# Scale columns and K projection in three chunks of three k-tiles, with the first layer norm's statistics reordered, in a diffusion transformer block

## The chip, the cores and the metric

One core of a Trainium2 chip runs the whole block as one program. The metric is device microseconds for one execution. The kernel before took 243.84 us (median of 3, 243.79 to 243.88). Chips and executions differ by some tenths of a microsecond, so each kernel was run beside the kernel before on the same chip. A profile adds the **span**, from the core's first instruction to its last. It is shorter than the time.

## The reference

```python
B, N, D = (2, 256, 1152);  F = 4 * D;  H = 2
mod = (silu(c) @ w_mod).reshape(B, 6, 1, D)
shift_a, scale_a, gate_a, shift_m, scale_m, gate_m = [mod[:, i] for i in range(6)]
h = layernorm(x) * (1 + scale_a) + shift_a
qkv = (h @ wqkv).reshape(B, N, 3, H, D // H)
...                                   # softmax attention, two heads
x = x + gate_a * (attn_out @ wo)
h2 = layernorm(x) * (1 + scale_m) + shift_m
return x + gate_m * (gelu(h2 @ w_fc1) @ w_fc2)
```

All tensors are bf16. D is 9 tiles of 128 ("k-tiles" as the contracted dimension). The 512 tokens are four tiles of 128, two for each batch element.

## The kernel before

Everything is recorded as units of work with their dependencies, and each engine runs its own queue in order. TensorE (PE) runs the units in the order in which the program states them; lists fix the first instructions of VectorE (DVE), ScalarE (ACT) and, in the changed kernel, GpSimd.

The stage in question is the first 34 us. It computes K before the shift is known: K of the scaled, unshifted rows. (The shift's part of K adds the same amount to all scores of a query, so softmax drops it.) The steps are: normalise four token tiles, transpose them on PE, compute the scale columns `silu(c) @ w_mod` as many matmuls of two columns, multiply (`hk`), and project. The scale weights come in chunks so that K can start on the first ones:

```python
KC = 4
for (ka, kb) in ((0, KC), (KC, KT)):            # scale columns 0..3, then 4..8
    for k0, k1 in ((0, 3), (3, 6), (6, 9)):
        dma(WSC[:, k0:k1, ka*P:kb*P], wmod_v[:, k0:k1, D + ka*P:D + kb*P], ...)
    for kt in range(ka, kb):
        dma(WK[:, kt, :], ...)
...
warm(7, "b")                                    # identity x zeros, 512 columns: keeps PE busy
for n, behind in ((1, "bn_ln1_1_1"), (1, "aggr_ln1_1"), (2, "veps_ln1_1"), (2, "rstd_ln1_1")):
    warm(n, behind, behind)                     # may start only after the named DVE or GpSimd step
xn_T(1)                                         # transposes of tile 1
sca(0, 3);  warm(1, "d");  sca(3, 6);  warm(1, "f", "aggr_ln1_2")
xn_T(0);  sca(6, 9);  xn_T(2, 0, 8)
...
k_pair(range(KT - 2), 3, 1, bank=1)             # the last pair of K columns, k-tiles 0..6
for k0 in range(0, KT, 3): ...                  # shift rows: silu(c) @ W_shift
copy_on("dve", SHR, ...)                        # their eviction
k17(0, KC, KT);  k17(1, 0, 2)                   # seven K matmuls beside it
...                                             # transpose the shift rows into columns (shT)
k_pair(range(KT - 2, KT), 3, 1, bank=1)         # the last pair's k-tiles 7, 8: four matmuls
k17(1, 2, KT)                                   # seven more; then Q, which needs the shift added
```

## Time and profile before

| | before |
|---|---|
| time | 243.84 us |
| time / span of the profiled run | 244.31 / 242.6 us |
| PE busy | 238.3 us, 98% of the span |
| tile 1 normalised / its transposes start on PE | 7.91 / 8.62 us |
| first K matmul | 11.55 us |
| first Q matmul | 33.20 us |

The lines are in the prediction. Note that the profiled run is a separate one, 0.47 us slower than the median; that matters below, too. A "start us, us" line of the chain gives start and length of a piece; in a timeline, "[0.28 <-X]" is idle time of the engine ahead of the instruction and what ended it. The first Q matmul is 0.216 us (one matmul of 512 columns) ahead of the first one recorded: its record is missing, while its weight load is there.

### The profile page before, as it was taken

The numbers are of one execution on the slowest core, as the hardware profiler recorded it, in microseconds if no ns is written. First come the engines' busy times: TensorE is split into PE (matmuls) and PEld (weight loads), VectorE is DVE, ScalarE is ACT, GpSimd is POOL, SyncE is SP. The second block draws the span as 40 slices with busy tenths as digits, with TensorE's granted clock in tenths as the row PEclk, the third lists the DMA queues.
The fourth block names the chain that finished last, engine by engine and source line by source line (L and its number), as shares of the span: only waits on it lengthen the run. The fifth ranks groups of instructions, "written<-read, shape, count | busy, mean of one in ns | idle before, by whom it ended". The sixth has DMA issues, their size and how long they took to land.

```text
span 242.6 us, 3989 instructions
## 1 busy us (share of the span) xinstructions
PE 238.3 (98%) x1717; PEld 146.4 (60%) x1727; DVE 120.0 (49%) x216; ACT 66.9 (28%) x136; POOL 21.7 (9%) x39
## 2 busy tenths in 40 slices
PE   7999999999999999999999999999999999999996
PEld 2688854557667666898444444444565665665664
DVE  3824379596988799789999600000012222211112
ACT  4730350345424207983233332222000000000000
POOL 1500000000021186400000000020000000000000
PEclk9999999999999999999999999999999999999999
DMA  6999999999994999999943488002000000000001
GB/s 237 330 383 394 388 392 389 397 412 408 390 355 138 349 385 393 390 320 394 329 145 87 165 301 331 0 16 85 0 16 19 16 16 19 16 16 16 19 17 32
DMA packets 29995, 51.57 MB, mean 213 GB/s; under 512 B 1431, under 2 KB 15643, under 8 KB 29979
## 3 DMA queue, kind: packets, MB, share of 16 engines
q1 hardware_dynamic: 29536, 50.14, 57.8%
q0 software_dynamic: 416, 1.19, 1.6%
q8 instruction: 13, 0.21, 0.4%
q14 instruction: 3, 0.02, 0.0%
q10 hardware_dynamic: 27, 0.00, 0.0%
HBM read 50.14 MB, written 1.19 MB: 212 GB/s over the span
## 4 chain that ended last, share of the span: by engine, by line
PE 98%; issue 0%; POOL 0%; DVE 0%; POOLq 0%
PE psum L688 96%; PE psum L691 2%; POOL arena L713 0%; DVE arena L1289 0%; DVE arena L1290 0%; POOL arena L712 0%; POOL arena L719 0%; POOL arena L717 0%; POOLq L1351 0%
## 5 line engine op out<-in xcount | busy, mean ns | idle before, releaser
L688 PE MATMUL psum<-arena 128*128 128x384 bf16 (+9 forms) x1628 | 235.0, 310 | 2.0 <-POOL arena L713 1.5
L688 PEld LDWEIGHTS psum<-arena 128*128 128x128 bf16 (+1 forms) x1638 | 141.1, 97 | 91.8 <-issue 4.7
L1081 DVE SCALAR_TENSOR_TENSOR arena<-arena 128x1152 f32<-128x1152 bf16 x32 | 44.7, 1413 | 0.6
L1289 DVE TENSOR_TENSOR arena<-psum,arena 128x384 f32<-128x384 f32 (+2 forms) x13 | 6.9, 527 | 68.3 <-PE psum L688 68.3
L1197 ACT ACTIVATE arena<-psum 128x512 bf16<-128x512 f32 (+1 forms) x44 | 22.4, 519 | 42.7 <-PE psum L688 42.7
L683 ACT ACTIVATE arena<-psum 128x512 bf16<-128x512 f32 (+6 forms) x37 | 19.5, 549 | 39.8 <-PE psum L688 38.5
L685 DVE CAST arena<-psum 128x512 bf16<-128x512 f32 (+3 forms) x13 | 8.1, 639 | 11.5 <-PE psum L688 11.5
L669 POOL DMA_DIRECT2D dit_scratch<-arena x3 | 1.8, 616 | 116.4 <-DVE arena L685 59.6
L1165 POOL TENSOR_TENSOR arena<-arena 128x384 f32<-128x384 f32 x12 | 10.9, 912 | 10.9 <-DVE arena L1164 9.3
L1108 DVE CAST arena<-psum 72x32 bf16<-72x32 f32 x1 | 0.2, 188 | 21.3 <-PE psum L688 21.3
L741 DVE BATCH_NORM_STATS2 arena<-arena 128x6 f32<-128x384 f32 (+1 forms) x18 | 9.5, 551 | 0.1
L1170 ACT ACTIVATE arena<-arena 128x1152 bf16<-128x1152 f32 x4 | 5.3, 1343 | 11.3 <-DVE arena L1169 11.3
L1164 DVE TENSOR_TENSOR arena<-psum,arena 128x384 f32<-128x384 f32 x12 | 6.5, 550 | 1.3 <-PE psum L688 1.2
L691 PEld LDWEIGHTS psum<-arena 128*128 128x128 bf16 (+1 forms) x89 | 5.9, 98 | 2.1 <-DMA arena<-in_c_dram 0.8
L691 PE MATMUL psum<-arena 128*128 128x128 bf16 (+1 forms) x89 | 7.1, 219 | 0.1
L1290 DVE TENSOR_TENSOR arena<-arena 128x384 bf16<-128x384 f32 (+2 forms) x13 | 6.9, 527 | 0.4
L1187 ACT ACTIVATE arena<-psum,arena 128x128 bf16<-128x128 bf16 x16 | 6.0, 455 | 1.5 <-PE psum L691 0.9
L1184 DVE TENSOR_SCALAR arena<-psum,arena 128x128 bf16<-128x128 bf16 x20 | 5.4, 336 | 1.9 <-PE psum L691 1.9
L1085 DVE STREAM_TRANSPOSE arena<-arena 128x1152 f32<-128x1152 f32 x4 | 5.5, 1368 | 0.0
L1088 DVE TENSOR_REDUCE arena<-arena 128x36 f32<-128x1152 f32 x4 | 5.4, 1346 | 0.0
L1011 ACT ACTIVATE arena<-psum,arena 128x256 bf16<-128x256 f32 x8 | 3.7, 472 | 1.3 <-PE psum L688 0.9
L745 POOL TENSOR_TENSOR arena<-arena 128x1 f32<-128x1 f32 x6 | 3.6, 596 | 1.6 <-DVE arena L744 1.6
(48 smaller groups left out, 45.3 us busy)
## 6 DMA issues: line engine op xcount, KB each, us to landing
arena<-in_w_fc_dram SPq DMA_DIRECT2D x9, 1152.0 KB, 7.1
arena<-in_w_fc_dram SPq DMA_DIRECT2D x4, 2592.0 KB, 17.4
arena<-in_wqkv_dram SPq DMA_DIRECT2D x18, 288.0 KB, 9.7
arena<-in_w_mod_dram SPq DMA_DIRECT2D x3, 1728.0 KB, 20.5
arena<-in_w_mod_dram SPq DMA_DIRECT2D x3, 864.0 KB, 13.0
arena<-in_w_mod_dram SPq DMA_DIRECT2D x9, 288.0 KB, 11.1
arena<-in_wqkv_dram SPq DMA_DIRECT2D x1, 2592.0 KB, 16.9
arena<-in_wo_dram SPq DMA_DIRECT2D x1, 2592.0 KB, 24.4
```

The source lines that it names most:

```text
L683: act(c_act(n), lambda e: e.activation(out=dst, in_=src, func=ACTF.Copy), [src], [dst], name)
L685: dve(c_dve_psum16(n) if psum16 else c_dve_psum32(n), lambda e: e.tensor_copy(dst, src), [src], [dst], name)
L688: S.instr(lambda e: e.matmul(o, lhsT=l, rhs=r, start=st, stop=sp, **kw), reads=[l, r], writes=[o])
L691: S.instr(lambda e: e.transpose(o, i_, idn), reads=[i_, idn], writes=[o])
L741: dve(550, lambda e, s=s, o=o: e.bn_stats(out=o, in_=s), [s], [o], "bn_%s_%d" % (tag, ci))
L1081: dve(1270, lambda e, w=w, s=s, acc=acc: e.scalar_tensor_tensor(out=acc, in0=w, scalar=s, in1=acc, op0=ALU.mult, op1=ALU.add), [w, s, acc] ...
L1164: dve(550, lambda e, o=o, ga=ga, x1c=x1c: e.tensor_tensor(out=x1c, in0=o, in1=ga, op=ALU.mult), [o, ga], [x1c], "wo_t1_%d_%d" % (t, ci))
L1165: S.op("pool", 930, lambda e, xs=xs, x1c=x1c: e.tensor_tensor(out=x1c, in0=x1c, in1=xs, op=ALU.add), reads=[x1c, xs], writes=[x1c], name=" ...
L1187: act(440, lambda e, o=o, dst=dst, s1=s1, s2=s2: e.activation(out=dst, in_=o, func=ACTF.Identity, scale=s1, bias=s2), [o, s1, s2], [dst], ...
L1197: act(c_act(ntok), lambda e: e.activation(out=dst, in_=o, func=ACTF.Gelu_apprx_tanh), [o], [dst], "gelu_%d_%d" % (f, tok0))
L1289: dve(c_dve_psum32(w), lambda e, o=o, gm=gm, t1=t1: e.tensor_tensor(out=t1, in0=o, in1=gm, op=ALU.mult), [o, gm], [t1], "fc2_t1_%d_%d" % ( ...
L1290: dve(c_dve_32(w), lambda e, t1=t1, x1c=x1c, ost=ost: e.tensor_tensor(out=ost, in0=t1, in1=x1c, op=ALU.add), [t1, x1c], [ost], "fc2_out_%d ...
```

## The change

The intent: smaller pieces, so that K can start earlier; tile 2's statistics ahead of all normalising, so that the three tiles are normalised in one go; and the last K pair ahead of the shift rows, whose weights arrive late.

```diff
-KC = 4
+KC = 3
-        for (ka, kb) in ((0, KC), (KC, KT)):
+        for (ka, kb) in ((0, KC), (KC, 2 * KC), (2 * KC, KT)):
...
-        for n, behind in ((1, "bn_ln1_1_1"), (1, "aggr_ln1_1"), (2, "veps_ln1_1"), (2, "rstd_ln1_1")):
+        for n, behind in (..., (2, "rstd_ln1_1"), (1, "bn_ln1_2_1"), (2, "bn_ln1_2_2")):
             warm(n, behind, behind)
+        sca(0, 3)
         xn_T(1)
-        sca(0, 3)
-        warm(1, "d")
         sca(3, 6)
-        warm(1, "f", "aggr_ln1_2")
         xn_T(0)
...   # one ACT copy of transposes more; the second half of the scale columns becomes two thirds,
...   # the last of them between the K matmuls of k-tile 5
         k_pair(range(KT - 2), 3, 1, bank=1)
+        k_pair(range(KT - 2, KT), 3, 1, bank=1)
...   # shift rows, eviction
         k17(0, KC, KT)
-        k17(1, 0, 2)
+        k17(1, 0, 1)
...   # shT
-        k_pair(range(KT - 2, KT), 3, 1, bank=1)
-        k17(1, 2, KT)
+        k17(1, 1, KT)
...
-            "dve": [..., "bn_ln1_2_1", "xn_1", "bn_ln1_2_2", "aggr_ln1_2", "veps_ln1_2", "xn_0", "var_ln1_3", "xn_2", ...
+            "dve": [..., "bn_ln1_2_1", "bn_ln1_2_2", "aggr_ln1_2", "veps_ln1_2", "xn_1", "xn_0", "xn_2", "var_ln1_3", ...
+            "pool": [..., "rstd_ln1_2", "mm_ln1_3", "rstd_ln1_3"],
```

More of the change, by code (lines that the diff above doesn't have):

```diff
@@ L801, in hk @@
             dst = HK[:, kt, b * 256:(b + 1) * 256]
-            s1 = ps32(1 if kt == 0 else 7, 2 * kt, 1) if kt in (0, KC) and b == 0 else SC1A[:, kt * 2 + b:kt * 2 + b + 1]
+            s1 = ps32(1 if kt == 0 else 7, 2 * kt, 1) if kt % KC == 0 and b == 0 else SC1A[:, kt * 2 + b:kt * 2 + b + 1]
             src = xslot(b, kt) if kt < KC else HX[:, kt, b * 256:(b + 1) * 256]
@@ L852, in build_kernel @@
         warm(7, "b")
-        for n, behind in ((1, "bn_ln1_1_1"), (1, "aggr_ln1_1"), (2, "veps_ln1_1"), (2, "rstd_ln1_1")):
+        for n, behind in ((1, "bn_ln1_1_1"), (1, "aggr_ln1_1"), (2, "veps_ln1_1"), (2, "rstd_ln1_1"), (1, "bn_ln1_2_1"), (2, "bn_ln1_2_2")):
             warm(n, behind, behind)
+        sca(0, 3)
         xn_T(1)
-        sca(0, 3)
-        warm(1, "d")
         sca(3, 6)
-        warm(1, "f", "aggr_ln1_2")
         xn_T(0)
@@ L868, in build_kernel @@
         xn_T_copy(0, 8, 9, "act")
+        xn_T_copy(0, 3, 4, "act")
         hk(2, 0, "act")
-        hk(3, 0, "act")
         def k_first(kt):
@@ L885, in build_kernel @@
             hk(kt, 1)
+        xn_T_copy(1, 3, 4, "dve")
         k_pair(range(KC), 0, 1)
-        k_pair(range(KC), 1, 1)
         def k17(b, ka, kb):
@@ L896, in build_kernel @@
         k17(0, 0, KC)
-        def k12(part):
-            kts = ((range(3), ()), (range(3, KC), range(KC)))[part]
-            S.unit("pe", sum(map(len, kts)) * c_mm(256), "k1_2_part%d" % part)
-            for half in range(2):
-                k_mm(kts[half], 4 + half, 1, KB[1][2], half)
         for kt in range(KT):
             if kt == 6:
-                k12(0)
-            mod_kt(WSC, kt, 0, "scb_%d" % kt, (KC, KT))
+                k_pair(range(KC), 1, 1)
+            mod_kt(WSC, kt, 0, "scb_%d" % kt, (KC, 2 * KC))
         hk(KC, 0)
-        sc1a(KC, KT)
-        for kt in range(KC, KT):
+        sc1a(KC, 2 * KC)
+        for kt in range(KC, 2 * KC):
             for b in range(2):
@@ L912, in build_kernel @@
                     hk(kt, b)
-        k12(1)
+        k_pair(range(KC), 2, 1)
+        for kt in range(KC, 2 * KC):
+            for b in range(2):
+                if kt == 2 * KC - 1:
+                    for k in range(6 * b, 6 + 3 * b):
+                        mod_kt(WSC, k, 0, "scc_%d" % k, (2 * KC, KT))
+                for i in range(4 - b):
+                    k_pair((kt,), i, b)
         for kt in range(KT):
@@ L916, in build_kernel @@
             dma(WSM[:, kt, :], wmod_v[:, kt, 4 * D:5 * D], P * D * 2, "ld_sm%d" % kt, run=2304)
-        for kt in range(KC, KT - 2):
+        hk(2 * KC, 0)
+        sc1a(2 * KC, KT)
+        for kt in range(2 * KC, KT):
             for b in range(2):
-                for i in range(4 - b):
-                    k_pair((kt,), i, b)
+                if kt > 2 * KC or b:
+                    hk(kt, b)
+        for b in range(2):
+            for i in range(4 - b):
+                k_pair((2 * KC,), i, b)
         for b in range(2):
@@ L974, in build_kernel @@
             "dve": ["zq4b", "c_half", "c_silu", "bn_ln1_1_0", "bn_ln1_1_1", "bn_ln1_1_2", "aggr_ln1_1", "veps_ln1_1", "bn_ln1_2_0",
-                    "bn_ln1_2_1", "xn_1", "bn_ln1_2_2", "aggr_ln1_2", "veps_ln1_2", "xn_0", "var_ln1_3", "xn_2", "hk_0_0", "sc1a_0", "sc1a_1", "hk_1_0", "xn_3",
-                    "hk_0_1", "hk_1_1", "hk_2_1", "hk_3_1", "hk_%d_0" % KC, "sc1a_4", "hk_%d_1" % KC] + ["hk_%d_%d" % (kt, b) for kt in range(KC + 1, KT) for b in range(2)],
-            "act": ["ld_c", "c_tanh", "sum_ln1_0", "sq_ln1_0", "sum_ln1_3", "sq_ln1_3", "xnT_cp0_4", "xnT_cp0_8", "hk_2_0", "hk_3_0",
+                    "bn_ln1_2_1", "bn_ln1_2_2", "aggr_ln1_2", "veps_ln1_2", "xn_1", "xn_0", "xn_2", "var_ln1_3", "hk_0_0", "sc1a_0", "sc1a_1", "hk_1_0",
+                    "xn_3", "hk_0_1", "hk_1_1", "hk_2_1", "xnT_cp1_3"]
+                   + [x for kt in range(KC, KT) for b in range(2) for x in (["hk_%d_%d" % (kt, b)] + (["sc1a_%d" % kt] if kt % KC == 0 and b == 0 else []))],
+            "act": ["ld_c", "c_tanh", "sum_ln1_0", "sq_ln1_0", "sum_ln1_3", "sq_ln1_3", "xnT_cp0_4", "xnT_cp0_8", "hk_2_0", "xnT_cp0_3",
                     "xnT_cp1_4", "xnT_cp1_8"],
+            "pool": ["ones", "ident", "nhalf", "rowpad0", "rowpad640", "mm_ln1_0", "rstd_ln1_1", "var_ln1_0", "rstd_ln1_0", "rstd_ln1_2",
+                     "mm_ln1_3", "rstd_ln1_3"],
         }
```

## The prediction

> **What bounds the kernel now.** I read the page first, then the chain of work that ended last in order of time, then the timeline of the first 35 us engine by engine, then DMA issues in narrow windows. The page says that PE carries everything:
>
> ```profile
> PE 238.3 (98%) x1717; PEld 146.4 (60%) x1727; DVE 120.0 (49%) x216; ACT 66.9 (28%) x136; POOL 21.7 (9%) x39
> ...
> PE 98%; issue 0%; POOL 0%; DVE 0%; POOLq 0%
> ```
>
> The change touches only the first 34 us: LN1, the scale columns, the K projection, the shift rows. There the chain (start us, length us, what) never leaves PE after 1.5 us:
>
> ```profile
> 4.96 3.82 PE psum L688 x11
> 8.78 0.50 PE psum L691 x9
> 9.29 0.83 PE psum L688 x25
> 10.11 0.08 issue
> 10.19 0.66 PE psum L691 x9
> 10.85 0.29 PE psum L688 x12
> 11.14 0.47 PE psum L691 x8
> 11.61 1.95 PE psum L688 x16
> 13.56 0.56 PE psum L691 x10
> 14.12 19.24 PE psum L688 x234
> ```
>
> The lines of L691 are the transposes of the normalised tiles; the x11 before them are warm-up matmuls (identity times zeros, 512 columns). So PE is busy before 8.6 us too, with work that computes nothing. Does it wait for LN1 at 8.62, where the first transpose starts? The DVE timeline says no:
>
> ```profile
> 6.43 1.01 DVE L741 BATCH_NORM_STATS2 arena<-arena 128x6 f32<-128x384 bf16 x2
> 7.35 0.56 DVE L762 TENSOR_SCALAR arena<-arena 128x1152 bf16<-128x1152 bf16 x1
> 7.83 0.55 DVE L741 BATCH_NORM_STATS2 arena<-arena 128x6 f32<-128x384 bf16 x1
> 8.42 0.24 DVE L742 BATCH_NORM_AGGREGATE arena<-arena 128x2 f32<-128x18 f32 x1
> 8.69 0.15 DVE L744 TENSOR_SCALAR arena<-arena 128x1 f32<-128x1 f32 x1
> 8.76 0.57 DVE L762 TENSOR_SCALAR arena<-arena 128x1152 bf16<-128x1152 bf16 x1
> ```
>
> L762 is the normalising of a tile: tile 1 is ready at 7.91, tile 0 at 9.33. PE takes them at 8.62 and 10.19. It comes late because its queue of warm-ups, each of them released long before, has to be run off first. Half of them run at the cold spacing (7.32 to 7.74, the weight loads 0.42 us apart):
>
> ```profile
> 7.32 0.15 PEld L688 LDWEIGHTS psum<-arena 128*128 128x128 bf16 x1 [0.28 <-DVE arena L741]
> 7.74 0.55 PEld L688 LDWEIGHTS psum<-arena 128*128 128x128 bf16 x3 [0.28 <-issue]
> ```
>
> So in this stretch **the end is set by the sum of PE's matmuls plus the few places where PE stands still**. From the start-to-start distances of single PE records after 8.62 us, what exceeds the usual distance is: 0.11 us at 11.55 (first K matmul; its K weights landed at 11.42), 0.04 at 12.24 (an ACT copy), 0.06 at 12.53 (next K weights), 0.12 at 20.10 (the first scaled tile of the second chunk), 0.05 at 31.76 (the eviction of the shift rows). A step of about 0.21 us at 10.19 and 33.41 is a matmul whose record is missing (1717 matmuls to 1727 loads), not a wait.
>
> **What the Trainium skill says.** "TensorE: Matmul & The Clock Gate", section "Wait — 56ns, not 53.3ns?": start to start is N/1.2 GHz while cold (426.7 ns for 512 columns) and N/2.4 plus 2.5 ns when warm (215.7 ns for 512, 55.6 for 128), never under about 25 ns. The trace agrees: 0.43 us cold, nine transposes in 0.50 us, 512-column warm-ups 215 ns apart after 7.97, two-column matmuls 26.5 ns apart, 256-column ones 109 ns. The same page, "What's actually happening", puts the change to full clock in a free-running window; the three runs within 0.09 us show no such scatter here. "DMA: Bandwidth & Descriptors", section "Specifications", asks for 512 B at least for line rate; the trace agrees only in part: the first scale chunk (1024 B rows) moves at 294 GB/s, the later weights (2304 B rows) at 392:
>
> ```profile
> 5.00:9.30 4.30, 4.30 (x27) 1.99 (x26) 4.16 (x12) 4.24 (x7) 2.47 (x6) 1.00 0.95 294
> ...
> 18.00:29.00 11.00, 11.00 (x136) 9.77 (x135) 4.88 (x17) 2.39 (x4) 0.00 (x0) 1.00 1.05 392
> ```
>
> **The change part by part.**
>
> *Warm-ups.* Out: "d" and "f", one each. In: one behind the second statistics part of tile 2 and two behind the third. The DVE finishes these at 7.44 and, with the normalising moved behind, about 7.9; PE reaches them at 8.62, so they start at once. Net one more matmul of 215 ns: **+0.215 us**. They all stand before the first useful matmul now, so scale columns start at 8.62 + 3 x 0.215 = 9.27.
>
> *Statistics of tile 2 first.* On DVE, third part at 7.35, aggregate and epsilon until 8.36, then the tiles 1, 0, 2 normalised until about 8.85, 9.4, 9.9. PE wants them at 9.51, 10.25, 10.99 (below). All come 0.6 us or more early: **0**. The gain that the reordering makes possible is eaten by the three warm-ups.
>
> *Three scale chunks instead of two.* The 81 two-column matmuls stay; nine of them (9 x 26.5 = 0.24 us) move from before the first K matmul to later: no change of the sum. PE then: 9.27 scale k 0..2 (9 x 26.5), 9.51 transposes tile 1 (0.50), 10.01 scale, 10.25 tile 0, 10.75 scale, 10.99 eight transposes of tile 2, 11.43 free. First scaling on DVE: now 0.25 us after the last first-column matmul (10.74 to 10.99), so 10.80 + 0.25 = 11.05, plus 0.36, plus 0.06 to PE: K starts at 11.47, a wait of 0.04. The ACT copies of the transposes start 0.26 us after the last transpose of tile 0, so 10.95, 0.06 later than now; the banks they free are wanted 0.08 us earlier: waits of 0.12 and 0.05 for the third and fourth K pair. The second K tile starts at 12.52, where it now starts at 12.53. Weights come sooner here, as the first chunk is 885 KB instead of 1180, so the 0.06 at 12.53 goes. Later: the scale ones wait for the last ACT copy of tile 3's transposes, about 0.04; the 0.12 at 20.10 goes down to about 0.01 at each of two places, because six K matmuls (0.65 us) stand there where five did.
>
> *Last K pair ahead of the shift rows.* Seven matmuls cover the rows' eviction as before. But after the transposing of the rows only 8 matmuls (0.87 us) stand before Q, where 11 (1.20 us) did. Shift columns and first two additions took from 32.01 to 32.94, plus 0.06 to PE, so 0.99 us: **a new wait of 0.12 us**.
>
> *Transfers.* Rows of scale weights shrink to 768 B: 3456 of them instead of 2304, so 216 per DMA engine instead of 144. From the rates, a 1024 B row cost 56 ns per engine and a 2304 B row 94. I take 42 ns for a 768 B row, an estimate between proportion to size from the smooth stretch (34) and no saving at all (56). 216 x 42 = 9.1 us against some 8.0 now: every later landing about 1 us later. The last shift weights landed at 28.96 and are used at 30.26; K's extra pair pushes the use 0.44 us on. The last Q weights land at 41.7 and are used at about 43.4; 42.8 still suffices. **0, with little to spare.**
>
> Sum of PE: +0.215 (one warm-up), minus the old waits that go (0.11 + 0.04 + 0.06 + 0.12 = 0.33), plus the new ones (0.04 + 0.17 + 0.04 + 0.02 + 0.12 = 0.39): **+0.28 us**. After Q nothing waits on anything but PE, so it is passed on whole: 243.84 + 0.28 = 244.1 us.
>
> **The rivals.** *The new order wins.* If the three new warm-ups only filled time in which PE would wait for the statistics, leaving out "d" and "f" (0.43 us) would count, and with the wait at 20.10 gone the time would be about 243.3. For it: that is the evident intent. Against: no warm-up now waits, and tile 1 would be normalised 0.65 us before PE wants it. *The short rows starve PE.* At 56 ns a row the stream is 4 us later; PE would wait for the third scale chunk (wanted at about 21) and for the last Q weights: 245 to 246.5. For it: the slow first chunk and a DMA busy without a gap until 58 us. Against: median rows in the trace are near proportional to size, and the slow part is the first microseconds. *A copy chain becomes the bound*: ACT has one copy more before tile 3's transposes, but it ends near 13.1 and the next need is at 14.15; I see at most 0.2 us more, 244.3.
>
> **Range and chances.** The sum is of terms of 0.05 to 0.2 us, each uncertain by half, so about 0.3 us either way; the first rival draws the low end, a part of the second the high end: 243.4 to 244.8. Two per cent is 4.9 us, more than all waits and warm-ups of the stage, so within 2% is all but sure: 0.98, with 0.01 on either side.
>
> **What would show it.** Three warm-ups 0.215 us apart between 8.62 and 9.27, then two-column matmuls; first K matmul at 11.4 to 11.6; no PE wait near 20; Q starting about 0.3 us later than the 33.2 of now; the last scale rows landing around 20 us. A first K matmul well before 11.4 would refute the warm-up count; PE waiting on a weights transfer anywhere would refute the DMA step.

## The result, and the profile after

The changed kernel took **244.38 us** (median of 4, 244.26 to 244.58); the kernel before, beside it, 243.86 (4 runs). The ratio is 1.0021, 95% interval 1.0003 to 1.0038. A ratio here is the mean of one kernel's fast runs over that of the other's in the same rounds, so not quite the ratio of the medians. The class is "same", and the time lies in the predicted range; the middle of the difference is 0.52 us where 0.28 was predicted.

The page of the changed kernel, engines' busy time and then the chain's shares, looks as before:

```profile
PE 238.2 (98%) x1719; PEld 146.4 (60%) x1728; DVE 120.5 (50%) x219; ACT 67.0 (28%) x136; POOL 21.2 (9%) x39
...
PE 98%; DVE 1%; issue 0%; POOL 0%; POOLq 0%
```

The chain of work in order of time, first stage:

```profile
4.88 4.26 PE psum L688 x23
9.15 0.63 PE psum L691 x9
9.78 0.22 PE psum L688 x9
9.99 0.52 PE psum L691 x9
10.52 0.21 PE psum L688 x9
10.73 0.47 PE psum L691 x8
11.20 1.97 PE psum L688 x16
...
32.93 0.29 DVE arena L972
33.22 0.08 issue
33.29 0.81 PE psum L688 x3
```

Two things are as foretold: transposes and two-column matmuls alternate in groups of nine, and a DVE line (L972, adding the shift) now stands in the chain ahead of Q. One is not: K starts near 11.1, well ahead of the predicted 11.47; by the prediction's own sign ("a first K matmul well before 11.4") that refutes its warm-up count. The timeline of PE's weight loads and the timeline of DVE say why:

```profile
6.38 0.15 PEld L688 LDWEIGHTS psum<-arena 128*128 128x128 bf16 x1 [0.28 <-DVE arena L741]
6.81 2.24 PEld L688 LDWEIGHTS psum<-arena 128*128 128x128 bf16 x17 [0.28 <-DVE arena L744]
9.10 0.51 PEld L691 LDWEIGHTS psum<-arena 128*128 128x128 bf16 x9
```

```profile
6.63 1.47 DVE L741 BATCH_NORM_STATS2 arena<-arena 128x6 f32<-128x384 bf16 x3
8.13 0.24 DVE L742 BATCH_NORM_AGGREGATE arena<-arena 128x2 f32<-128x18 f32 x1
8.40 0.15 DVE L744 TENSOR_SCALAR arena<-arena 128x1 f32<-128x1 f32 x1
8.47 1.71 DVE L762 TENSOR_SCALAR arena<-arena 128x1152 bf16<-128x1152 bf16 x3
```

PE went over from 0.43 to 0.22 us a warm-up: the first one at full rate starts at 7.0 us, not at 8.0 as in the trace of before. So the warm-ups were through at 8.77 and the first nine scale matmuls at 9.01, and PE then stood still for 0.09 us until tile 1 was normalised (9.04). The warm-ups are not what bounds this run up to here; LN1 on DVE is.

The transfers: with 768 B rows the scale weights moved faster than expected. The second and third piece of the first chunk, 24 rows for each of the 16 DMA engines, landed 0.88 us after the one before: 37 ns a row where 42 was assumed. The windows view (the last two columns are DMA share and GB/s) has, for a stretch that holds the end of the token load (landed at 6.17) and most of the first chunk, and for the later weights:

```profile
5.20:9.30 4.10, 4.10 (x27) 1.89 (x26) 3.96 (x12) 4.04 (x7) 2.25 (x5) 1.00 1.04 355
...
20.00:29.00 9.00, 9.00 (x105) 8.07 (x104) 4.10 (x13) 2.39 (x4) 0.00 (x0) 1.00 1.06 391
```

The last scale rows landed at 20.15, the last Q weights at 42.29 against 41.74 before: 0.55 us later, and PE waits for none of them.

**A puzzle.** PE's last weight load is at 240.03 in this trace and at 240.15 in that of before. PE ends 0.12 us earlier, yet the span is 243.1 instead of 242.6. (The two profiled runs took 244.37 and 244.31 us: this pair of traces differs by 0.06 us in time, not by 0.52.) The difference in span lies behind the last matmul. Of the last store (16 KB; us from issue to landing in the last column) the two traces say, first before, then changed, where an instruction transfer also falls into the same window:

```profile
out_dram<-arena SPq DMA_DIRECT2D x1, 16.0 KB, 1.4
```

```profile
q14 instruction: 1, 0.01, 1.6%
...
out_dram<-arena SPq DMA_DIRECT2D x1, 16.0 KB, 2.0
```

An instruction fetch of 8 KB starts at 241.68 in the changed kernel and holds one DMA engine for 0.59 us, while the last store is under way. In the kernel before it starts at 243.62, behind everything. The change adds three transfers to SyncE's queue, so SyncE comes to the point of that fetch earlier. Was the 0.52 us nothing but this?

### The profile page after: what moved, and what is told of

Its sections match the earlier page's. It is cut to its first block, busy times and chain, and to the rows that moved or that the text cites. A ratio compares the mean times of both kernels' runs of the same rounds, so it can differ in the third digit from the quotient of the medians.

```text
span 243.1 us, 4000 instructions
## 1 busy us (share of the span) xinstructions
PE 238.2 (98%) x1719; PEld 146.4 (60%) x1728; DVE 120.5 (50%) x219; ACT 67.0 (28%) x136; POOL 21.2 (9%) x39
## 3 DMA queue, kind: packets, MB, share of 16 engines
q0 software_dynamic: 416, 1.19, 1.5%
HBM read 50.14 MB, written 1.19 MB: 211 GB/s over the span
## 4 chain that ended last, share of the span: by engine, by line
PE 98%; DVE 1%; issue 0%; POOL 0%; POOLq 0%
PE psum L688 96%; PE psum L691 2%; DVE arena L972 0%; POOL arena L713 0%; DVE arena L1296 0%; DVE arena L1297 0%; POOL arena L712 0%; DVE arena L963 0%; POOL arena L717 0%; POOLq L1358 0%
```

## The experiments

Theory T: the extra time arises in the last store, through the fetch. Rival P: it is PE's, as the prediction summed it. Each kernel ran in five rounds; the kernel before had nine runs on the same chip: 244.00 us for e1 to e4, 243.93 for e5 to e8, 244.18 for e9 to e11 (medians). All eleven kernels gave correct results.

**e1: the kernel before with three transfers more.**

```diff
-for k0 in range(0, KT, 3):
-    dma(WSH[:, k0:k0 + 3, :], ...)
+for k0, k1 in ((0, 2), (2, 3), (3, 5), (5, 6), (6, 8), (8, 9)):
+    dma(WSH[:, k0:k1, :], ...)
```

> The kernel before, with its shift weights loaded by six transfers instead of three: the SyncE queue gets the three more transfers that the change also adds, and nothing else of the change. Theory T (the extra time of the change arises at the very end: three more SyncE instructions bring an instruction fetch of 8 KB, which fell behind the last store in the kernel before, onto the last store): 244.3 to 244.5, an instruction transfer of 8 KB between 241 and 242 us, the last store 2.0 us to its landing instead of 1.4. Rival P (the extra time is TensorE's, one warm-up more and a wait before Q): 243.8 to 243.95, as before.

Measured: 244.13 us (243.84 to 244.48), ratio 1.0007 (0.9993 to 1.0020). The fetch did move onto the last store, at 241.48:

```profile
q14 instruction: 1, 0.01, 1.2%
...
out_dram<-arena SPq DMA_DIRECT2D x1, 16.0 KB, 1.8
```

Yet the median rose by 0.13 us only, within the noise, not by the 0.3 to 0.5 us that theory T needs (the interval alone would allow up to 0.5). The reason shows when span and time are set side by side: in all five runs the time is 1.23 to 1.32 us longer than the span, while in the nine runs of before beside it the time is 1.70 to 1.78 us longer. What the span gains, the end behind it loses. (Spans are on record to 0.1 us, so these differences are good to 0.05.)

**e2: the changed kernel with three transfers less.**

```diff
-for k0 in range(0, KT, 3):
-    dma(WMODR[:, k0:k0 + 3, :], ...)
+dma(WMODR, wmod_v[:, :, 2 * D:4 * D], ...)
 # and the loads of WSM[:, 7] and WSM[:, 8] as one
```

> The changed kernel with three transfers less on SyncE, later in the program (the three loads of the gate and shift rows as one, the last two pieces of the scale of the second norm as one), so as many as before. Theory T: the fetch goes behind the last store again, last store 1.4 us, time 243.7 to 243.95. Rival P: 244.3 to 244.4, as the changed kernel. If both are true in part, in between: 0.3 us above the kernel before is what the blind sum gave to TensorE.

Measured: 244.36 us (244.17 to 244.84), ratio 1.0017 (1.0004 to 1.0029). The last store is back at 1.4 us and the fetch at 243.48, the profiled span fell to 242.4, and the time stayed where the changed kernel's was. **Theory T falls as the account of the difference**; it explains the span, and of the time only a part in some runs. That part can be read from the traces. From PE's last weight load to the end of the timed run (time less the last load) it is 4.09 to 4.17 us in eleven of the 13 traces, with the fetch behind the last store or on it, but 4.34 and 4.35 us in those of the changed kernel and of e3. In these two the fetch on the store took 0.59 us, in the other five with the fetch on the store 0.42 to 0.49; the last store took 2.0 and 2.1 us instead of 1.8. For e3:

```profile
out_dram<-arena SPq DMA_DIRECT2D x1, 16.0 KB, 2.1
```

So a long fetch went with about 0.2 us more of time; what makes it long, and how often it is long in runs without a trace, is not known.

In the trace of e2, too, the clock was full early (from 5.7 us), K starts at 11.07 and PE's last load is at 240.04. In e1, with an early clock as well, it is at 239.84: at like clock the changed kernel's PE ends 0.20 us later.

**e3: the changed kernel without its three new warm-ups.**

```diff
-for n, behind in (..., (2, "rstd_ln1_1"), (1, "bn_ln1_2_1"), (2, "bn_ln1_2_2")):
+for n, behind in (..., (2, "rstd_ln1_1")):
```

> The changed kernel without the three new warm-up matmuls. If TensorE was bound by the warm-ups there, as predicted, three times 0.215 us go, less what it then waits for tile 1 (normalised about 9.0): 0.4 to 0.6 us faster than the changed kernel, 243.8 to 244.0, with the late store still in it. Rival: the warm-ups only fill a wait for LN1, and the time stays at 244.3.

Measured: 244.33 us (244.26 to 244.45), ratio 1.0014 (1.0001 to 1.0026). No gain. In PE's weight-load timeline the time of the warm-ups turned into a wait for the normalising:

```profile
9.13 0.51 PEld L691 LDWEIGHTS psum<-arena 128*128 128x128 bf16 x9 [0.95 <-DVE arena L762]
```

K starts at 11.10, as with them. With the clock early (full from 6.2 us here), the three warm-ups fill a wait and cost nothing. That is the prediction's first step refuted, for such runs. (The time of this trace's run holds the 0.2 us of the long fetch; the judgement rests on PE's last load, 240.06 here and 240.03 with the warm-ups.)

**e4: e2 and e3 together.**

> Both: no new warm-ups and three transfers less. If the two causes are separate they add up: 243.1 to 243.5, faster than both kernels. If the fetch is the whole of it: 243.7 to 243.9.

Measured: 244.20 us (244.15 to 244.82), ratio 1.0016 (1.0003 to 1.0030). Neither cause adds anything, so nothing adds up. The five runs form two groups, 244.15 to 244.20 and 244.68 to 244.82; the profiled one is of the slower. Up to 92 us its PE agrees with e2's; then PE waits at the second layer norm:

```profile
93.30 0.51 PEld L691 LDWEIGHTS psum<-arena 128*128 128x128 bf16 x9 [0.32 <-ACT arena L1178]
...
98.88 0.10 PEld L688 LDWEIGHTS psum<-arena 128*128 128x128 bf16 x1 [0.16 <-DVE arena L1192]
```

The gate rows, which go through a round trip to device memory on GpSimd's queue, landed at 84.11 there and at 82.98 in e2, and LN2 on DVE started by as much later. In the three traces in which they landed at 83.95 or later (e4, e7, e9) PE lost about 0.5 us so (first Q matmul to last weight load 207.42 to 207.45 us); in the others, up to 83.5, nothing (206.95 to 206.96). That is read from traces; no run moved the gate rows on purpose. This hits kernels irrespective of the change, and may be a good part of the scatter of 0.2 to 0.7 us within each set of runs; how often it strikes a run without a trace cannot be seen.

**e5: the kernel before again, as a kernel under test.**

> The kernel before, unchanged, as a kernel under test: a second trace of it, and a measure of the noise. Ratio to itself 1.000 within 0.001. If TensorE gets its full clock early (before 7 us) in this trace, the transposes of tile 1 start at about 8.08, waiting for the DVE, and K at about 11.3; if late (near 7.8 us), at 8.6 and 11.55 as in the first trace.

Measured: 244.11 us (243.82 to 244.12), ratio 1.0002 (0.9989 to 1.0014). That is the noise: about 0.3 us either way in one interval. The clock was full from 7.3 us, in between; K starts at 11.35. Before K, PE waits here (0.24 us) and in e1 (0.41 us) for the second piece of the first scale chunk, which landed at 9.48 and 9.35. The line of e1:

```profile
9.39 0.41 PEld L688 LDWEIGHTS psum<-arena 128*128 128x128 bf16 x13 [0.41 <-DMA arena<-in_w_mod_dram]
```

**e6: the changed kernel again.**

> The changed kernel, unchanged: 0.3 to 0.5 us over the kernel before (ratio 1.0013 to 1.0021). If the clock comes late, the sum of the prediction holds in the form it was written in: scale columns at 9.27, K at 11.47. If early: tile 1's transposes wait for the DVE until 9.10, K at 11.07, and TensorE's last matmul about 0.2 us later than in the kernel before with an early clock.

Measured: 244.25 us (244.10 to 244.41), ratio 1.0009 (0.9995 to 1.0023). Here the clock came late (full from 7.6 us), and the trace has the predicted form: the warm-ups end about 9.14, tile 1 has been normalised since 8.86, and PE goes on without a wait, with the transposes at 9.38 (the chain puts a piece where the one before it has ended).

```profile
9.52 0.52 PE psum L691 x9
10.04 0.22 PE psum L688 x9
10.26 0.52 PE psum L691 x9
```

K starts at 11.33, 0.26 us later than with the early clock.

**e7: the last K pair put back behind the shift rows.**

```diff
 k_pair(range(KT - 2), 3, 1, bank=1)
-k_pair(range(KT - 2, KT), 3, 1, bank=1)
...
+k_pair(range(KT - 2, KT), 3, 1, bank=1)
 k17(1, 1, KT)
```

> The changed kernel with one part undone: the last K pair is again behind the transposing of the shift rows. If the wait before Q is the new wait it was taken for: Q's first matmul 0.12 to 0.14 us earlier against the start of K than in the changed kernel (21.87 instead of 22.01 us from first K to first Q matmul), time 0.14 us less, as far as the noise lets it be seen. If the wait merely moves elsewhere (the shift weights landing late, wanted 0.44 us earlier): no gain.

Measured: 244.30 us (243.82 to 244.50), ratio 1.0009 (0.9997 to 1.0022). From first K to first Q matmul PE took 21.87 us instead of 22.01: the wait of 0.14 us is gone, as expected. The time cannot show it; this trace fell among those with late gate rows.

**e8: the kernel before without the warm-ups "d" and "f".**

```diff
-warm(1, "d")
-warm(1, "f", "aggr_ln1_2")
```

> The kernel before without the two warm-ups that the change leaves out, and nothing else. If they cost what they last: 0.43 us less, and the rival that counted on them is right in its mechanism. I expect 0 to 0.1 us: without them TensorE comes to the third piece of the first scale chunk and to the first K weights before they land (10.5 and 11.4), so K starts at 11.2 to 11.55 either way.

Measured: 244.03 us (243.75 to 244.37), ratio 1.0002 (0.9989 to 1.0014). No gain in time, as expected. In the trace (full clock from 5.1 us) K starts at 11.15 and PE's last load is at 239.64, 0.20 us ahead of e1's with its like clock, so a gain of up to 0.2 us is not excluded. In their place PE waits for scale weights (line of its weight-load timeline):

```profile
10.31 0.38 PEld L688 LDWEIGHTS psum<-arena 128*128 128x128 bf16 x12 [0.22 <-DMA arena<-in_w_mod_dram]
```

So the rival that counted 0.43 us for these two would have been wrong by half or more.

**e9: three chunks, most of the rest of the change undone.** DVE's old order, no new warm-ups, the last pair behind. ("d" and "f" stay out, the first scale columns stay ahead of tile 1's transposes, and ACT's and GpSimd's lists stay new.)

```diff
-"bn_ln1_2_1", "bn_ln1_2_2", "aggr_ln1_2", "veps_ln1_2", "xn_1", "xn_0", "xn_2", "var_ln1_3"
+"bn_ln1_2_1", "xn_1", "bn_ln1_2_2", "aggr_ln1_2", "veps_ln1_2", "xn_0", "xn_2", "var_ln1_3"
 # and the edits of e3 and e7
```

> The changed kernel with its other parts undone: three scale chunks stay, but tile 1 is normalised ahead of tile 2's last statistics as before, the three new warm-ups are out, and the last K pair is again behind the transposing of the shift rows. From the traces: tile 1's transposes at 8.1 with an early clock, then the wait goes over to tile 2 (normalised at 10.5), K at about 10.95 instead of 11.07; first K to first Q matmul 21.87 us as without the early pair; so TensorE ends 0.2 to 0.25 us ahead of the changed kernel and level with the kernel before, within 0.1 us: time 243.9 to 244.1. If the chunks themselves were the gain and the rest its loss, it would be 0.3 us and more ahead of the kernel before.

Measured: 244.30 us (243.99 to 244.61), ratio 1.0010 (0.9997 to 1.0022), in a trace with late gate rows. The time is above the 243.9 to 244.1 that was expected. The transposes of tile 1 begin at 8.22 (expected 8.1), but K at 11.11, where 10.95 was expected: PE waits for tiles 0 and 2 instead. And here the shift weights are late:

```profile
30.11 0.25 PEld L688 LDWEIGHTS psum<-arena 128*2 128x2 bf16 x12 [0.51 <-DMA arena<-in_w_mod_dram]
```

The last of them landed at 30.07, while PE, without the early pair, had come to the shift rows at 28.86. This is what moving the pair ahead protects against; about 0.28 us of PE time were lost there. From first K to first Q matmul it took 21.95 us, where 21.87 was expected.

**e10: the kernel before with the early pair alone.**

```diff
 k_pair(range(KT - 2), 3, 1, bank=1)
+k_pair(range(KT - 2, KT), 3, 1, bank=1)
...
-k_pair(range(KT - 2, KT), 3, 1, bank=1)
 k17(1, 2, KT)
```

> The kernel before with one part of the change alone: the last K pair ahead of the shift rows (7 matmuls instead of 11 between the transposing of the shift rows and Q). The wait before Q alone: 11 matmuls covered 1.20 us, 7 cover 0.76, and the shift columns and two additions need 0.99, so 0.22 to 0.25 us more from first K to first Q matmul (21.87 instead of 21.64), time 0.2 us over the kernel before. If something else decides when Q starts (the Q weights): no difference.

Measured: 244.15 us (244.09 to 244.40), ratio 1.0007 (0.9994 to 1.0019). From first K to first Q 21.89 us, 0.25 more than the 21.64 of before; the weight load ahead of Q waits for the DVE's shift addition:

```profile
33.01 0.98 PEld L688 LDWEIGHTS psum<-arena 128*128 128x128 bf16 x6 [0.35 <-DVE arena L968]
```

Up to K this kernel is the kernel before. In this trace the second scale piece landed at 9.11, PE did not wait for it, and K starts at 11.13.

**e11: the changed kernel a third time.**

> The changed kernel once more, to narrow its difference in time: so far 0.52 us on one chip (4 runs each) and 0.32 on another (5 to 9). By the prediction's sum 0.28; by the traces' positions of TensorE 0.16 (early clock) to 0.28 (late). Expected here 0.2 to 0.45, and a span that is 0.5 us longer still, with an end behind the span that is 0.5 us shorter.

Measured: 244.22 us (244.16 to 244.61), ratio 1.0012 (0.9999 to 1.0026). Over the span the time is 1.21 to 1.28 us longer, in the runs of before 1.69 to 1.78, as expected.

No version beat the kernel before beyond the noise; where the traces show one wait gone, another stood right behind it.

## Why the prediction was right or wrong, point by point

The positions of PE in the traces, in us (full clock: start of the first matmul at full rate; K to Q: first to first matmul):

| trace | full clock | K starts | K to Q | last load of PE |
|---|---|---|---|---|
| before | 8.0 | 11.55 | 21.64 | 240.15 |
| before again (e5) | 7.3 | 11.35 | 21.67 | 239.98 |
| before with six shift loads (e1) | 5.1 | 11.27 | 21.62 | 239.84 |
| before with the early pair (e10) | 7.2 | 11.13 | 21.89 | 239.98 |
| changed | 7.0 | 11.07 | 22.01 | 240.03 |
| changed again (e6) | 7.6 | 11.33 | 22.01 | 240.30 |
| changed a third time (e11) | 5.0 | 11.11 | 22.01 | 240.07 |

- **What bounds the stage: right for the trace that was read, too narrow as a rule.** With a late clock, warm-ups hold PE up and LN1 is done in time. With an early one PE waits for LN1 in the changed kernel, and in the kernel before for LN1 and then for scale weights (e1: 0.64 and 0.41 us). The step that failed is the sentence that three runs within 0.09 us show no scatter of the clock. The clock did scatter: full rate began between 4.6 and 8.0 us over 13 traces. Three runs were too few to show it, and the profiled run itself, with the latest clock of all, took 244.31 us, outside these three. So the prediction read its waits from an execution that was not typical. (A smaller slip: the warm-ups are not cold by half there but by nine of 13.)
- **Warm-ups, "+0.215 us": wrong for early clocks.** e3 shows them free there. For late clocks e6's trace has them on PE's path as described; a run without them and with a late clock did not occur, so that half is read from a trace, not shown by removal.
- **Statistics first, "0": right for K's start, for another reason with an early clock.** Tile 1 is then normalised about a microsecond later (9.04 instead of 8.0 to 8.2) and PE waits for it, but K starts no later. e9 with the old order and without the new warm-ups starts K at 11.11, as the changed kernel does.
- **From K to Q: right.** The prediction's terms between the first K matmul and Q are 0.24 (scale matmuls moved there), 0.17 less 0.10 (ACT copies, and the small waits that go), 0.04, 0.02 less 0.12, and 0.12 (the wait before Q): 0.37 us. Measured 22.01 less 21.64: 0.37. The waits for ACT are 0.12 and 0.05 us in the changed trace, the one before Q is 0.14, that at 20.10 is gone.
- **K's start: right in sign; the size, without a late clock, is luck.** Predicted 0.08 us earlier. The changed kernel has 11.07 to 11.11, the kernel before's first stage 11.13 (e10), 11.27 (e1) and 11.35 (e5), so the gain is 0.02 to 0.28 us, and much of it hangs on when the first scale chunk lands: its second piece came at 9.11, 9.35 and 9.48 there, by 8.74 in the changed kernel's traces, whose pieces are smaller. The prediction had neither this wait nor the one for LN1.
- **Transfers, "0, with little to spare": right.** No wait for weights in the changed kernel's three traces. The delay of the Q weights was 0.55 us, not 1. The 56 ns for a 1024 B row is too high for the pieces behind the first: its window also holds the end of the token load and the chunk's slow first piece, while the second and third piece of that chunk (24 rows an engine) landed after 1.01 and 1.26 us, 42 and 53 ns a row. e9 shows how little was to spare.
- **The sum.** That what is lost before Q is passed on whole is right in the ten traces without late gate rows: from the first Q matmul to the last weight load it is 206.95 to 206.96 us in each of them. In the three others PE does wait for something else after Q, which the prediction had ruled out. At like clock PE ends 0.20 to 0.23 us later (e2 and e11 against e1). Against e10, with the 0.25 us of its early pair taken off (an estimate: 239.73), it is 0.30 to 0.34. At 7.6 us, with before interpolated between its traces of 7.3 and 8.0, it is about 0.24. Predicted 0.28. The time ratios of the changed kernel, 1.0021, 1.0009 and 1.0012, average 1.0014, or 0.34 us. This lies within the interval of the first comparison (0.07 to 0.93 us), whose 0.52 us needs no second cause. What made up the rest was not separated; candidates seen in traces are the long fetch (0.2 us), the gate rows (0.5 us) and the clock.
- **Not foreseen at all:** the fetch on the last store. It lengthens the span by 0.45 us, by 0.7 where it is long, and shortens the end behind it by about 0.5, so only the long one is seen in the time.

Of the rivals, "the new order wins" fell (e3: what the warm-ups leave is a wait; e8: of 0.43 us at most 0.2 could be left), "the short rows starve PE" did not come true, and the ACT copies cost the 0.17 that the main sum gave them.

## What to carry to other kernels

When filler work stands on the bounding engine, ask what would stand behind it, at the earliest and at the latest clock, before counting it as time to be won: here two kinds of warm-up could be taken out, and neither gave anything beyond the noise. Look also whether the profiled run took the usual time before you read its waits as the usual ones. Work moved ahead of one wait is cover taken from another, and can be priced by counting the matmuls left in front of the next wait, to a few hundredths of a microsecond. And for differences under 1 us compare times, not spans: what falls behind the last instruction is in the one and not in the other.

## What the Trainium skill lacked or had wrong

- "TensorE: Matmul & The Clock Gate", section "What's actually happening", has a free-running window of about 3.4 us and calls the transition point variable by 500 ns either way. Over 13 traces here it lay between 4.6 and 8.0 us, a spread of 3.4 us, which fits the page's window length, and its own note of 6, 11 or 14 cold matmuls for one kernel, but not its 500 ns.
- The same section's advice not to fit to a cold count is borne out, but the page does not say that a data wait behind the warm-ups can absorb the scatter: K started within 0.04 us in the changed kernel for full clock at 5.0 and at 7.0 us.
- "Runtime: NRT & Kernel Launch", section "Instruction fetch mechanics", lacks that the fetching of instructions can delay a kernel's own transfers: with an 8 KB fetch of 0.42 to 0.49 us on one DMA engine the last store took 1.8 us instead of 1.4, with one of 0.59 us 2.0 to 2.1.
- No page says that the time behind the span varies with it: 1.67 to 1.81 us for kernels with the fetch behind the last store, 1.19 to 1.32 for those with it on the store.
- "DMA: Bandwidth & Descriptors", section "Specifications", has line rate from 512 B rows. By the landings, the second and third piece of the first scale chunk moved at 389 and 312 GB/s with 1024 B rows (kernel before), at 335 with 768 B rows (changed kernel), and the long rows at 391 to 392. So neither is at the long rows' rate throughout, though both are above 512 B; row length alone does not explain these. (The 294 and 355 GB/s of the windows above mix in the end of the token load.)
